# Reordering the normalisation of q and k in an attention and soft-MoE kernel: q squared one quad earlier, transposes moved forward, norm moved on VectorE

## The chip, the cores and the metric

The kernel runs on one core of a Trainium2 chip. The metric is device time in microseconds (us) of one execution. A profile comes from one execution, and its span is about 1.8 us shorter than that execution's device time (301.9 against 303.69 us before the change). Unless said otherwise, all runs compared are fast.

## The reference, cut to what matters

```python
def rmsnorm(x, g):
    rms = np.sqrt(np.mean(x * x, axis=-1, keepdims=True) + 1e-06)
    return x / rms * g
# attention: batch 8, 12 heads, 448 tokens, head size 64
q_n, k_n = rmsnorm(q, g_q), rmsnorm(k, g_k)
attn = softmax(q_n @ k_n.T / sqrt(64));  x = attn @ v        # x: 3584 x 768
# soft MoE: 8 experts of 4 slots, 768 -> 1024 -> 768
logits = x @ phi
slot_input = softmax(logits over tokens).T @ x
slot_out = per expert: relu(slot_input @ w1) @ w2
out = softmax(logits over slots) @ slot_out
```

Only the factors 1/rms and the order in which they are made concern us.

## The kernel before

The attention works on quads (four heads), 24 of them, three to a batch. Quad Q is scored while k and q of quad Q+1 are transposed and those of quad Q+2 are normalised. In the trace of this kernel each engine's instructions stand in the order of the program text (seen from 118 to 127 us): in the turn that begins at 120.59 us TensorE runs score 0 (120.59), 12 ov matmuls (120.97), score 1 (121.44), 8 of ov (121.82), score 2 (122.13), 8 of ov (122.51), 7 transposes of q (122.76) and score 3 (123.78). One turn of the loop, with cuts:

```python
if on: score(Q, 0)               # PE: two matmuls; ACT: exp
if ahead:
    square(Q + 2, 0)             # ACT: q*q
    if Q: square(Q + 2, 1, True) # POOL: k*k
ov(Q - 1, 1, 7, 10)              # PE: attn @ v, half 1 of the quad before
moe_evac(moe)                    # DVE: copy of x transposed (xT)
score(Q, 1); ov(Q - 1, 1, 10, 12)
rowsum(Q + 2, 0)                 # DVE: sum of q*q
# if mb (last quad of a batch): logits on PE, exp on ACT
score(Q, 2); ov(Q - 1, 1, 12, 14)
trans(Q + 1, 0); evac(Q + 1, 0)  # PE: 7 transposes of q; DVE: evacuation
rowsum(Q + 2, 1)                 # DVE: sum of k*k
score(Q, 3)
norm(Q - 1, 1)                   # DVE: divides half 1 of ov, frees the accumulator
trans(Q + 1, 1); vcopy(Q + 1)    # PE: 8 transposes of k; POOL: casts of v
rsqrt(Q + 2)                     # ACT: Ln, Exp = "factor pass", 28 columns
scaleqk(Q + 2, 0); scaleqk(Q + 2, 1)   # POOL
score(Q, 4); ov(Q, 0, 0, 4)      # waits for norm(Q - 1, 1): one ov accumulator
evac(Q + 1, 1)                   # DVE: two copies, partitions 0-63 and 64-127
score(Q, 5); ov(Q, 0, 4, 7)
# if mb: moe_sin: expert sums and transposes of e on PE, sacc and eT on DVE
score(Q, 6); norm(Q, 0); moe_x(Q - 1)
```

PSUM holds two score tiles, one ov accumulator and two slots ("misc") for transposes and small tiles. A score must wait until the exp two scores back has emptied its slot: score 3 waited 0.47 us for exp 1 in the turn above, and started at 123.78 us, 0.96 us after that exp did.

The softmax here doesn't subtract the row's maximum and nothing guards it: scores larger than these inputs give would overflow.

## Time and profile before

| | before |
|---|---|
| device time, median of 3 (range) | 303.25 us (302.88 to 305.39) |
| span of the profiled run | 301.9 us |
| attention part / expert and output tail | 229 / 73 us |
| plain quad, norm to norm of half 1 | 8.12 us |
| third quad (with expert sums) | 10.2 to 10.5 us |

A fourth run of this kernel (303.02 us) came with the runs of the changed kernel; the medians below include it. Times of quads are read as the distance between two starts of the norm of half 1 on VectorE (DVE) in the timeline. "Third quad" here is the stretch that follows the norm in a quad that ends a batch, because the expert sums lie in it. The first norm of half 1 is that of quad 0; it runs in turn 1 of the loop, so some texts call it the norm of quad 1, and a stretch between two norms is called by the turn in which it ends. Two lines from the table of waits of the kernel before; the columns are who waited, for whom, us in total, times, longest:

```profile
DVE ss L186 <- ACT arena L180: 27.6, 19, 2.3
...
ACT ss L190 <- DVE ss L186: 12.6, 24, 3.8
```

VectorE's sum waits for Square on ScalarE (ACT), and ScalarE's factor pass waits for the sum. The change aims at the first.

### The profile page before, as it was taken

To read this page: it belongs to the slowest core of one execution; us is meant where nothing else is said; L and a number is where in the kernel's file an instruction comes from. 1 tells how busy PE (TensorE), PEld (TensorE's weight loads), DVE (VectorE), ACT (ScalarE), POOL (GpSimd) and SP (SyncE) were. 2 spreads that over 40 slices of the span, in tenths; PEclk is the share of its full clock that TensorE was granted. 3 is DMA by queue.
4 is the path that set the end of the run, shared out by engine and by line. 5 is a ranking of instruction groups with operands and counts; after the bars stand their busy time and mean duration, and the time that the engine had idled before them with its cause. 6 is when DMAs were issued, how large, how long until landed. Compare 5 with 4: busy or idle time off the path is not lost.

```text
span 301.9 us, 8426 instructions
## 1 busy us (share of the span) xinstructions
PE 219.0 (73%) x3564; PEld 157.8 (52%) x3564; DVE 189.8 (63%) x315; ACT 193.3 (64%) x270; POOL 167.4 (55%) x187
## 2 busy tenths in 40 slices
PE   7568878687877867787788589686976756689900
PEld 2244556455655645565556456554745746654300
DVE  5765777887777788777767877877555300038800
ACT  4388988778878877887867889687771000026700
POOL 0389999767968885978776689779502100000000
PEclk9969999999999999999979999999998555555555
DMA  6996999999999899999994998939999999209996
GB/s 194 280 285 175 243 265 251 272 241 252 244 243 267 236 212 270 220 258 280 232 236 129 227 263 205 226 104 154 212 211 214 209 212 211 55 2 396 405 414 247
DMA packets 44918, 69.81 MB, mean 231 GB/s; under 512 B 3920, under 2 KB 36688, under 8 KB 44880
## 3 DMA queue, kind: packets, MB, share of 16 engines
q1 hardware_dynamic: 29184, 44.05, 48.9%
q0 software_dynamic: 15376, 25.22, 46.1%
q8 instruction: 28, 0.46, 0.6%
q14 instruction: 10, 0.08, 0.1%
q10 hardware_dynamic: 320, 0.00, 0.1%
HBM read 83.46 MB, written 11.01 MB: 313 GB/s over the span
## 4 chain that ended last, share of the span: by engine, by line
PE 36%; DVE 33%; ACT 17%; issue 5%; DMA 3%; POOL 1%; SPq 0%; POOLq 0%; DVEq 0%
DVE ss L186 13%; ACT arena L243 11%; PE ov L256 11%; PE sc L242 8%; DVE arena L267 7%; DVE eT L310 5%; ACT arena L180 4%; PE hTp L444 4%; PE soTp L453 4%; PE op L483 3%; DVE arena L223 3%; PE sinp L298 2%; DMA arena<-in_v_dram 2%; PE op L484 2%; DVE rd L266 2%
## 5 line engine op out<-in xcount | busy, mean ns | idle before, releaser
L243 ACT ACTIVATE arena<-sc 128x896 bf16<-128x896 f32 x168 | 146.2, 916 | 28.0 <-PE sc L242 27.7
L242 PE MATMUL sc<-arena 128*128 128x448 bf16 x336 | 93.2, 360 | 10.2 <-ACT arena L243 9.1
L198 POOL TENSOR_TENSOR arena<-arena,rs 128x896 bf16<-128x896 f32 x47 | 79.6, 1714 | 35.0 <-issue 19.3
L256 PE MATMUL ov<-arena 128*128 128x65 bf16 (+1 forms) x1344 | 67.2, 199 | 40.7 <-DVE arena L267 40.6
L256 PEld LDWEIGHTS <-arena 128*128 128x128 bf16 x1344 | 59.1, 99 | 71.3 <-DVE arena L267 43.5
L186 DVE TENSOR_REDUCE ss<-arena 128x14 f32<-128x896 f32 x48 | 51.8, 1080 | 28.1 <-ACT arena L180 27.6
L487 ACT ACTIVATE wown<-op,arena 128x768 f32<-128x768 f32 x14 | 12.4, 899 | 42.3 <-PE op L484 42.3
L178 POOL TENSOR_TENSOR arena<-arena 128x896 f32<-128x896 f32 x21 | 35.4, 1687 | 0.2
L267 DVE TENSOR_TENSOR arena<-ov,rd 128x512 bf16<-128x512 f32 x48 | 33.2, 691 | 1.7
L242 PEld LDWEIGHTS <-arena 128*128 128x128 bf16 x336 | 25.7, 98 | 14.5 <-issue 11.5
L227 DVE COPY arena<-qkTp 64x896 bf16<-64x896 bf16 x48 | 29.6, 616 | 0.6
L216 PE MATMUL qkTp<-ident,arena 128*128 128x128 bf16 x360 | 28.7, 223 | 0.4 <-DVE arena L198 0.4
L180 ACT ACTIVATE arena<-arena 128x896 f32<-128x896 f32 x27 | 25.4, 942 | 3.4 <-DMA arena<-in_q_dram 2.2
L216 PEld LDWEIGHTS <-arena 128*128 128x128 bf16 x360 | 23.2, 100 | 5.8 <-issue 0.7
L223 DVE TENSOR_SCALAR arena<-qkTp,gg 128x896 bf16<-128x896 bf16 x24 | 16.2, 675 | 5.4 <-PE qkTp L216 5.3
L266 DVE RECIPROCAL rd<-ov 128x8 f32<-128x8 f32 x48 | 10.0, 207 | 13.3 <-PE ov L256 13.2
L489 DVE TENSOR_SCALAR wown<-op,arena 128x768 f32<-128x768 f32 x14 | 14.1, 1016 | 4.6 <-PE op L484 4.4
L281 DVE COPY arena<-xTp 128x1024 bf16<-128x1024 bf16 x24 | 16.3, 680 | 1.1 <-PE xTp L278 1.1
L483 PE MATMUL op<-arena,eT 32*128 32x512 bf16 x28 | 16.0, 616 | 1.4 <-ACT wown L487 0.7
L205 POOL CAST arena<-arena 128x384 bf16<-128x384 f32 x24 | 12.1, 505 | 8.4 <-PE ov L256 8.3
L190 ACT ACTIVATE ss<-ss,eps 128x28 f32<-128x28 f32 (+1 forms) x26 | 8.2, 316 | 12.6 <-DVE ss L186 12.6
L278 PEld LDWEIGHTS <-arena 128*128 128x128 bf16 x192 | 12.9, 99 | 5.6 <-DVE arena L267 1.1
(62 smaller groups left out, 207.8 us busy)
## 6 DMA issues: line engine op xcount, KB each, us to landing
wown<-in_moe_w_dram POOLq DMA_DIRECT2D x11, 1536.0 KB, 14.2
arena<-in_q_dram SPq DMA_DIRECT2D x24, 448.0 KB, 6.5
arena<-in_k_dram SPq DMA_DIRECT2D x24, 448.0 KB, 8.1
out_dram<-wown SPq DMA_DIRECT2D x12, 768.0 KB, 9.0
arena<-in_moe_w_dram POOLq DMA_DIRECT2D x5, 1536.0 KB, 17.8
arena<-in_v_dram SPq DMA_DIRECT2D x48, 128.0 KB, 6.5
arena<-in_v_dram SPq DMA_DIRECT2D x48, 96.0 KB, 7.5
out_dram<-wown SPq DMA_DIRECT2D x4, 384.0 KB, 8.9
```

The lines of the kernel that those rows point to most:

```text
L178: nc.gpsimd.tensor_tensor(sq(t), r, r, op=MUL)
L180: nc.scalar.activation(out=sq(t), in_=r, func=ACTF.Square)
L186: nc.vector.reduce_sum(sss[Q][:, t], sq(t).rearrange("p (r d) -> p r d", d=D), axis=AX)
L198: (eng or nc.gpsimd).tensor_tensor(qkn(Q, t).rearrange("p s (r d) -> p s r d", r=2), raw(Q)[:, t].rearrange("p r (s d) -> p s r d", d=D), ...
L216: nc.tensor.transpose(pts[t][:, i], qkn(Q, t)[:, s], ident)
L223: nc.vector.tensor_scalar(qT(Q).rearrange("p w (s c) -> p w s c", s=NT), pt[:, :, :NT], gg, None, op0=MUL)
L227: nc.vector.tensor_copy(kT(Q)[r, :, hh].rearrange("p w (s c) -> p w s c", s=NT), pt[r, :, 1 - hh:8 - hh])
L242: nc.tensor.matmul(sc[:, j, :S], kT(Q)[:, w].rearrange("p h c -> p (h c)")[:, kc:kc + 128], qT(Q)[:, w], start=True, stop=True)
L243: nc.scalar.activation(out=at("attn", i).rearrange("p (h c) -> p h c", h=2), in_=sc[:, :, :S], func=ACTF.Exp, scale=0.125)
L256: nc.tensor.matmul(ovs[w][:, c, o0:o0 + n], attn(i)[:, C0[c]:C0[c] + 128], mov, start=(first and i == lo and c % 2 == 0), stop=(i in (6, 13)),
L267: nc.vector.tensor_tensor(xq(Q).rearrange("p c (h w d) -> p c h w d", h=2, w=2)[:, :, :, w], o[:, :, :, :D], rd.to_broadcast([128, 4, 2, D ...
L483: nc.tensor.matmul(op[:, 0], eTtok(j, s), so4[r, :512], start=True, stop=True, tile_position=tp)
```

## The change

Its intent: the sum of q no longer waits for a Square of the same quad, the transposes come early enough for their evacuations to be out of the way, and the norm, which frees the ov accumulator, no longer stands behind the sum of k. The diff, cut to its core (the split of the raw buffer into four q slots and three k slots, the index change of the factor tiles to Q+t, and one weight load moved from quad 20 to 21 are left out):

```diff
-    for t in range(2):              # prologue
-        square(0, t)
-        rowsum(0, t)
-    for t in range(2):
-        rsqrt(0, t, t + 1)
+    square(0, 0)
+    rowsum(0, 0)
+    square(0, 1)
+    rsqrt(0, 0, 1)
+    square(1, 0)
+    rowsum(1, 0)
+    rowsum(0, 1)
+    rsqrt(1)                        # k of quad 0 and q of quad 1
 ...
-    for t in range(2):
-        square(1, t)
-        rowsum(1, t)
-        rsqrt(1, t, t + 1)
-        scaleqk(1, t)
+    scaleqk(1, 0)
+    square(1, 1)
+    square(2, 0)
+    rowsum(1, 1)
+    rowsum(2, 0)
+    rsqrt(2)
+    scaleqk(1, 1)
 ...
         score(Q, 0)
+        square(Q + 3, 0)
-        square(Q + 2, 0)
         square(Q + 2, 1, ...)
+        trans(Q + 1, 0); evac(Q + 1, 0)
         ov(Q - 1, 1, 7, 10); moe_evac(moe)
+        scaleqk(Q + 2, 0)
         score(Q, 1); ov(Q - 1, 1, 10, 12)
+        trans(Q + 1, 1); evac(Q + 1, 1)
+        rowsum(Q + 3, 0)
-        rowsum(Q + 2, 0)
         score(Q, 2); ov(Q - 1, 1, 12, 14)
-        trans(Q + 1, 0); evac(Q + 1, 0)
-        rowsum(Q + 2, 1)
         score(Q, 3); norm(Q - 1, 1)
-        trans(Q + 1, 1)
         vcopy(Q + 1)
-        rsqrt(Q + 2); scaleqk(Q + 2, 0); scaleqk(Q + 2, 1)
+        rowsum(Q + 2, 1)
         score(Q, 4); ov(Q, 0, 0, 4)
-        evac(Q + 1, 1)
+        rsqrt(Q + 3, ...); scaleqk(Q + 2, 1)
```

More of the change, by code (lines that the diff above doesn't have):

```diff
@@ L68, in place @@
         places[name] = (off, elems, n)
-    place("raw", 2 * 2 * 2 * NT * D, 3)
+    place("rawq", 2 * 2 * NT * D, 4)
+    place("rawk", 2 * 2 * NT * D, 3)
     place("sq", 2 * 2 * 2 * NT * D, 1)
@@ L102, in loadw, with raw @@
         nc.gpsimd.dma_start(out=wt[i], in_=wsrc(i))
-    def raw(Q):
-        return at("raw", Q).bitcast(F32).rearrange("p (t r x) -> p t r x", t=2, r=2)
+    def raw(Q, t):
+        return at(("rawq", "rawk")[t], Q).bitcast(F32).rearrange("p (r x) -> p r x", r=2)
     def load(Q, t):
         src = (q, k)[t][Q // QB, Q % QB * 4:Q % QB * 4 + 4].rearrange("h t d -> (h t) d")
-        nc.sync.dma_start(out=raw(Q)[:, t], in_=src.rearrange("(r p s) d -> p r (s d)", r=2, s=NT))
+        nc.sync.dma_start(out=raw(Q, t), in_=src.rearrange("(r p s) d -> p r (s d)", r=2, s=NT))
     def vraw(Q):
@@ L174, in square @@
     def square(Q, t, pool=False):
-        r = raw(Q)[:, t].rearrange("p r x -> p (r x)")
+        r = raw(Q, t).rearrange("p r x -> p (r x)")
         if pool:
@@ L182, in rowsum, with rsqrt @@
     def rowsum(Q, t):
-        if t == 0:
-            sss[Q] = small.tile([128, 2, 2 * NT], F32, tag="ss", name="ss")
-            rss[Q] = small.tile([128, 2, 2 * NT], F32, tag="rs", name="rs")
-        nc.vector.reduce_sum(sss[Q][:, t], sq(t).rearrange("p (r d) -> p r d", d=D), axis=AX)
-    def rsqrt(Q, t0=0, t1=2):
-        ss, rs = sss[Q][:, t0:t1], rss[Q][:, t0:t1]
+        n = Q + t
+        if n not in sss:
+            sss[n] = small.tile([128, 2, 2 * NT], F32, tag="ss", name="ss")
+            rss[n] = small.tile([128, 2, 2 * NT], F32, tag="rs", name="rs")
+        nc.vector.reduce_sum(sss[n][:, t], sq(t).rearrange("p (r d) -> p r d", d=D), axis=AX)
+    def rsqrt(n, t0=0, t1=2):
+        ss, rs = sss[n][:, t0:t1], rss[n][:, t0:t1]
         nc.scalar.activation(out=ss, in_=ss, func=ACTF.Ln, scale=1.0 / D, bias=eps)
@@ L196, in scaleqk @@
     def scaleqk(Q, t, eng=None):
-        rs = rss[Q][:, t].rearrange("p (r s) -> p s r", r=2)
+        rs = rss[Q + t][:, t].rearrange("p (r s) -> p s r", r=2)
         (eng or nc.gpsimd).tensor_tensor(qkn(Q, t).rearrange("p s (r d) -> p s r d", r=2),
-                                         raw(Q)[:, t].rearrange("p r (s d) -> p s r d", d=D),
+                                         raw(Q, t).rearrange("p r (s d) -> p s r d", d=D),
                                          rs.to_broadcast([128, NT, 2, D]), op=MUL)
@@ L325 @@
     evac(0, 1)
-    for t in range(2):
-        square(1, t)
-        rowsum(1, t)
-        rsqrt(1, t, t + 1)
-        scaleqk(1, t)
+    scaleqk(1, 0)
[5 more added lines that the diff above has]
+    scaleqk(1, 1)
     vcopy(0)
-    WQ = [0, 2, 4, 6, 9, 11, 13, 16, 18, 20, 20, 21, 22, NQ, NQ]
+    WQ = [0, 2, 4, 6, 9, 11, 13, 16, 18, 20, 21, 21, 22, NQ, NQ]
     for Q in range(NQ + 2):
@@ L345 @@
             score(Q, 0)
+        if Q + 3 < NQ:
+            square(Q + 3, 0)
         if ahead:
-            square(Q + 2, 0)
-            if Q:
-                square(Q + 2, 1, True)
+            square(Q + 2, 1, Q > 0)
+        if Q + 1 < NQ:
+            trans(Q + 1, 0)
+            evac(Q + 1, 0)
         if 0 <= Q - 1 < NQ:
@@ L353 @@
             moe_evac(moe)
+        if ahead:
+            scaleqk(Q + 2, 0)
         if on:
@@ L358 @@
             ov(Q - 1, 1, 10, 12)
-        if ahead:
-            rowsum(Q + 2, 0)
-            if Q == 0:
-                square(2, 1)
+        if Q + 1 < NQ:
+            trans(Q + 1, 1)
+            evac(Q + 1, 1)
+        if Q + 3 < NQ:
+            rowsum(Q + 3, 0)
         if mb is not None:
@@ L369 @@
             ov(Q - 1, 1, 12, 14)
-        if Q + 1 < NQ:
-            trans(Q + 1, 0)
-            evac(Q + 1, 0)
-        if ahead:
-            rowsum(Q + 2, 1)
         if on:
@@ L380 @@
         if Q + 1 < NQ:
-            trans(Q + 1, 1)
             vcopy(Q + 1)
         if ahead:
-            rsqrt(Q + 2)
-            scaleqk(Q + 2, 0)
-            scaleqk(Q + 2, 1)
+            rowsum(Q + 2, 1)
         for q3 in (2, 3) if Q == 0 else (Q + 3,):
@@ L393 @@
             ov(Q, 0, 0, 4)
-        if Q + 1 < NQ:
-            evac(Q + 1, 1)
+        if ahead:
+            rsqrt(Q + 3, 0 if Q + 3 < NQ else 1)
+            scaleqk(Q + 2, 1)
         if on:
```

## The prediction

> **What bounds the kernel now.** I read the page's first two parts, then the table of stretches, the chain of waits, and last the timeline of one quad (a quad is four heads; 24 of them pass through the loop). No engine is full:
>
> ```profile
> PE 219.0 (73%) x3564; PEld 157.8 (52%) x3564; DVE 189.8 (63%) x315; ACT 193.3 (64%) x270; POOL 167.4 (55%) x187
> ...
> PEclk9969999999999999999979999999998555555555
> ```
>
> The shares mix an attention part (to about 229 us) with a tail of expert layers and output that the change leaves alone, 73 us long. In the table of stretches the attention part alone, 60 to 203 us, shows ScalarE busy 116.45 of 143 us, TensorE 110.69, VectorE 110.03, GpSimd 109.66: four engines near 80%, none at its limit, so the order in which they wait decides. The chain of waits between 118 and 128 us shows that order for one plain quad:
>
> ```profile
> 117.66 0.70 DVE arena L267
> 118.36 0.05 issue
> 118.41 0.66 PE ov L256 x16
> 119.07 0.39 PE sc L242 x2
> 119.46 0.02 issue
> 119.48 2.60 ACT arena L243 x3
> 122.08 0.85 ACT arena L180
> 122.93 0.02 issue
> 122.95 1.09 DVE ss L186
> 124.04 0.59 DVE arena L223
> 124.63 0.99 DVE ss L186
> 125.62 0.13 DVE rd L266
> 125.75 0.02 issue
> 125.77 0.70 DVE arena L267
> 126.47 0.05 issue
> 126.52 0.67 PE ov L256 x16
> 127.19 0.39 PE sc L242 x2
> ```
>
> It is a ring: norm (L267) to norm takes 125.77 - 117.66 = 8.11 us. The norm frees the one ov accumulator, 16 ov matmuls run, score 5 follows, then exp 5, exp 6, exp 0 of the next quad and Square of q on ScalarE, then on VectorE sum of q, evacuation of q (L223), sum of k, norm. In that ring ScalarE waits twice:
>
> ```profile
> 125.66 0.32 ACT L190 ACTIVATE ss<-ss,eps 128x28 f32<-128x28 f32 x1 [0.32 <-DVE ss L186]
> 126.07 0.23 ACT L191 ACTIVATE rs<-ss 128x28 f32<-128x28 f32 x1
> 126.20 0.90 ACT L243 ACTIVATE arena<-sc 128x896 bf16<-128x896 f32 x1
> 127.60 2.60 ACT L243 ACTIVATE arena<-sc 128x896 bf16<-128x896 f32 x3 [0.51 <-PE sc L242]
> ```
>
> 0.32 us before the factor pass (Ln and Exp) and 0.51 us after exp 5: 0.83 us of 8.12. So ScalarE needs 7.29 us a quad and the most that any reordering can win in a plain quad is 0.83 us. Every third quad (the last of a batch) also holds the expert sums and the 1.90 us copy to eT (L310). In the chain three quads take 26.7 us (norm at 90.96 to norm at 117.66), so such a quad takes 26.7 - 2 x 8.12 = 10.4 us.
>
> [...] each engine's timeline has the kernel's order, and the norm at 125.77 stands behind a sum that it does not need. So I may follow queues by hand. [...] Here the gaps repeat, and there is one ov accumulator and two slots each for score tiles and small PSUM tiles. [...] the 48 sums last 1073 to 1087 ns whatever GpSimd does.
>
> **The change part by part.** (a) No work is added or removed in a steady quad: still two squares, two sums, one Ln/Exp pair of 28 columns, the same transposes. (b) Square of q is done for quad Q+3, of k for Q+2, and the pass takes both together; it moves from behind exp 3 to behind exp 4. (c) On TensorE the transposes of q follow score 0 and those of k follow score 1 (both followed score 2 and 3). (d) On VectorE the built order becomes: evacuation of q, copy of xT (L281), evacuation of k (two copies), sum of q, norm of half 1, sum of k, norm of half 0. Before: xT, sum q, evacuation q, sum k, norm, evacuation k, norm. So the norm passes only the sum of k; the sum of q still precedes it, and the evacuation of k (1.26 us), which used to follow, now precedes it too.
>
> What (b) wins: the old ring is cut, as the sum of q no longer waits for this quad's Square in time to matter. What (c) and (d) build is a new ring. The factor pass stands on ScalarE before exp 5 and needs the sum of k. In VectorE's order that sum comes after everything from the evacuation of q on. The evacuation needs the q transposes, which stand behind score 0, and score 0 needs the score slot that exp 5 of the previous quad frees. Each hop with a duration from this trace, start to start:
> 1. score 0 (two matmuls) until the transposes start: 0.38 (119.76 to 120.14, sc to the next transposes).
> 2. seven transposes until the evacuation of q starts: 0.59 (141.94 to 142.53, VectorE waiting).
> 3. evacuation of q: 0.59 (123.96 to 124.55).
> 4. xT copy 0.68 plus 0.06 to wake TensorE (norm end 126.46 to ov 126.52): 0.74. The k transposes need this: the small PSUM tiles have two slots, and theirs is the slot that the xT tile holds until it is copied. The built program has such a wait of TensorE on VectorE there.
> 5. eight transposes until the evacuation of k starts: 0.61 + 0.04 = 0.65.
> 6. two copies: 1.29 (11.31 to the next sum at 12.60).
> 7. sum of q: 0.99 (124.55 to 125.54).
> 8. norm: 0.23 + 0.61 = 0.84 (125.54, 125.77, 126.38).
> 9. sum of k 1.09 plus 0.03 to wake ScalarE: 1.12.
> 10. Ln and Exp until exp 5 starts: 0.54 (125.66 to 126.20).
> 11. exp 5 until score 0 may start: 0.96 (122.82 to 123.78).
> Sum 8.69 us, against 8.12 now: +0.57 per plain quad. The same way of adding gives the old ring exactly: 2.50 (exp 5, 6, 0) + 0.97 + 1.01 + 0.59 + 0.99 + 0.23 + 0.75 + 0.50 + 0.58 = 8.12, which is why I trust it. Other paths fit inside: score 5 is ready 1.14 us after the norm's end while exp 5 is released only at 1.59; ScalarE then idles about 1.4 us ahead of each factor pass.
>
> Third quads: sacc, eT and the norm of half 0 come after the sum of k. Counted from the end of the norm of half 1, the evacuation of the next q starts 3.52 us later in a plain quad, but 5.50 in a third one (16 ov 0.06, sacc 2.31, eT 2.73, norm 4.65 to 5.50, taken from the third quad at 134.6 to 140.1). That is +1.98, and about 0.1 for the memset of e: 8.69 + 2.08 = 10.77, against 10.4.
>
> Sum over the 20 quads from exp 5 of quad 0 (23.53) to exp 5 of quad 20 (201.20), 177.7 us now, of which I take 1.6 as a dip of the granted clock near 153 us that may come again: 14 x 8.69 + 6 x 10.77 + 1.6 = 187.9, so +10.2. Quad 21 has no sum of q any more (8.69 - 0.99 = 7.70; it now takes 8.7, held by GpSimd with two weight loads): -1.0. The prologue: k's first factors now wait also for q of quad 1, and the first exps for q of quad 2; following the queues I get about +1.0. The tail is unchanged: the weight loads that follow quad 21 still have some microseconds to spare. Total +10.2: 303.25 becomes about 313; I round down to 312.5, since each hop may overlap a little more than I allow.
>
> **The rivals.** First, the intent works: the Square-to-sum wait (27.6 us in 19 waits in the table of waits) goes and ScalarE runs through at 7.29 us; 0.83 x 14 plus about 1.5 x 6 saves some 20 us, giving 283. For it: that wait is the largest of VectorE, and the norm comes one sum earlier relative to k. Against it: the ring above, which is made of queue order and not of speed. Second, a draw: if the k transposes do not wait for the xT copy (hop 4 shrinks by about 0.35), or the two copies overlap, the ring is 8.2 to 8.3 and the time 304 to 307. Third, GpSimd becomes the bound: per quad 3 x 1.69 + 1.8 of casts, plus 0.94 for a weight load, 6.9 to 7.8 us; below 8.69, so it would only cap the first rival. Fourth, transfers: q must now be there a quad earlier, by my count 11.7 us after its issue; the landings of q and k have a median of 7.3 and a maximum of 13.3, so a rare wait is possible, and adds perhaps 1 to 3 us.
>
> **Range and chances.** An error of 0.25 us in the ring is 20 x 0.25 = 5 us, a different prologue or clock dip 2 us; so 306 to 318. The 2% lines lie at 297.2 and 309.3. Below 309.3 needs a ring under about 8.5; below 297.2 needs the ring not to exist. Slower 0.73, same 0.21, faster 0.06.
>
> **What would show it.** Right: norm to norm of half 1 near 8.7 us in plain quads; the wait of the Ln for the sum of k grows from 0.32 to above 1 us per quad (now 12.6 us in 24 waits, 4.9 of it between 60 and 203 us; then above 25); the wait of the sum of q for Square all but vanishes; in the chain the evacuations of q and k, xT and both sums stand in a row, and exp time shrinks to one exp per quad. Wrong: the norm of half 1 following the k evacuation with no sum before it, k transposes running ahead of the xT copy, or ScalarE with no repeated gap ahead of the factor pass.

## The result, and the profile after

| | before | after |
|---|---|---|
| device time, median of 4 (range) | 303.13 us (302.88 to 305.39) | 313.22 us (311.51 to 315.0) |
| span of the profiled run | 301.9 us | 309.7 us |
| plain quad | 8.12 us | 8.37 to 8.40 us |
| third quad | 10.2 to 10.5 us | 10.5 to 10.7 us |
| first norm of half 1 (turn 1 of the loop) | 29.92 us | 32.55 us |

The ratio is 1.0316 (95% interval 1.0239 to 1.0393). Here and below a ratio is the mean time of one kernel's fast runs over that of the kernel before in the same rounds, so it is not quite the ratio of the medians.

The kernel became 3% slower, though it does the same work. The page of the changed kernel:

```profile
PE 225.3 (73%) x3564; PEld 160.1 (52%) x3564; DVE 196.3 (63%) x315; ACT 191.9 (62%) x268; POOL 165.2 (53%) x187
```

The numbers of instructions are those of the kernel before, but for two fewer on ScalarE, so no work was added, though TensorE and VectorE show 3% more busy time: it is the order. The table of waits:

```profile
ACT ss L193 <- DVE ss L189: 31.2, 23, 4.8
...
DVE ss L189 <- ACT arena L181: 3.0, 2, 2.8
```

The wait that the change aimed at fell from 27.6 to 3.0 us, as intended. In exchange ScalarE's wait for the sums, ahead of the factor pass, grew from 12.6 to 31.2 us. The chain of waits of one plain quad shows why (columns: start, us, engine, tile, line):

```profile
125.60 0.69 DVE arena L270
126.29 1.00 DVE ss L189
...
127.32 0.33 ACT ss L193
...
127.95 0.81 ACT arena L246
...
128.81 0.54 PE sc L245 x2
129.35 0.39 PE qkTp L219 x7
129.74 0.48 PE ov L259 x12
130.22 0.38 PE sc L245 x2
130.60 0.24 PE ov L259 x8
130.84 0.46 PE qkTp L219 x8
...
131.32 0.62 DVE arena L230
...
132.61 1.09 DVE ss L189
...
133.97 0.69 DVE arena L270
```

Read from the top: norm (L270), sum of k (L189), factor pass (L193 and one more), exp 5 (L246), score 0 of the next quad (L245), transposes of q (L219), then on TensorE's own queue 12 ov matmuls, score 1 and 8 ov matmuls, transposes of k, evacuation of k (L230, two halves), sum of q, reciprocal, norm. 133.97 - 125.60 = 8.37 us. Before, this chain had three exps and a Square in a row; now it has one exp. It is a ring that the new order closes: ScalarE's queue has the factor pass ahead of exp 5, VectorE's queue has the sum of k behind the evacuations, and TensorE's queue has the transposes behind score 0.

Where the 7.8 us between the two profiled spans are, by the starts of the norms (differences of the two timelines):

| stretch | before | after | difference |
|---|---|---|---|
| until the first norm of half 1 | 29.92 | 32.55 | +2.6 |
| 13 plain quads, without their excess | 105.6 | 109.0 | +3.4 |
| 6 third quads | 62.3 | 63.9 | +1.6 |
| excess of long quads (see below) | 1.6 | 2.7 | +1.1 |
| turns 21 to 23 | 24.3 | 23.1 | -1.2 |
| last quad and tail | 78.3 | 78.5 | +0.2 |

Long quads are single quads that take 1.3 to 1.6 us more than their kind while the granted clock is low. In the table of stretches of the changed kernel (columns: us, busy time of PE, PEld, DVE, ACT, POOL, granted clock, DMA share, GB/s), this is the stretch of the first of two such quads, which took 9.70 and 9.73 us (32.6 to 52.0 us):

```profile
30.00:40.00 10.00, 8.27 (x103) 5.87 (x101) 6.70 (x11) 7.91 (x11) 8.76 (x10) 0.83 1.08 231
```

The granted clock is 0.83 there, and 1.00 from 50 us on. The profiled run was the fastest of the four (311.51 us), so the median of 10.1 us above before holds some 2 us that this trace does not show.

### The profile page after: what moved, and what is told of

The parts are those of the page before. It is cut to its first block, busy times and chain, and to the rows that moved or that the text cites. A ratio compares the mean times of both kernels' runs of the same rounds, so it can differ in the third digit from the quotient of the medians.

```text
span 309.7 us, 8398 instructions
## 1 busy us (share of the span) xinstructions
PE 225.3 (73%) x3564; PEld 160.1 (52%) x3564; DVE 196.3 (63%) x315; ACT 191.9 (62%) x268; POOL 165.2 (53%) x187
## 4 chain that ended last, share of the span: by engine, by line
PE 42%; DVE 33%; ACT 9%; issue 7%; DMA 3%; POOL 1%; SPq 0%; ACTq 0%; POOLq 0%
DVE ss L189 11%; PE ov L259 11%; PE sc L245 10%; DVE arena L270 7%; ACT arena L246 6%; PE qkTp L219 6%; DVE arena L230 6%; DVE eT L313 5%; PE hTp L451 3%; PE op L490 3%; PE soTp L460 3%; DVE rd L269 2%; PE sinp L301 2%; DMA arena<-in_k_dram 2%; PE op L491 2%
## 5 line engine op out<-in xcount | busy, mean ns | idle before, releaser
L246 ACT ACTIVATE arena<-sc 128x896 bf16<-128x896 f32 x168 | 144.0, 919 | 17.5 <-PE sc L245 15.6
L201 POOL TENSOR_TENSOR arena<-arena,rs 128x896 bf16<-128x896 f32 x47 | 81.4, 1733 | 57.5 <-ACT rs L194 48.1
L245 PE MATMUL sc<-arena 128*128 128x448 bf16 x336 | 94.8, 365 | 13.0 <-ACT arena L246 9.4
L259 PEld LDWEIGHTS <-arena 128*128 128x128 bf16 x1344 | 60.1, 99 | 54.3 <-DVE arena L270 35.4
L189 DVE TENSOR_REDUCE ss<-arena 128x14 f32<-128x896 f32 x48 | 51.6, 1081 | 3.7 <-ACT arena L181 3.0
L245 PEld LDWEIGHTS <-arena 128*128 128x128 bf16 x336 | 26.5, 100 | 25.4 <-issue 20.7
L230 DVE COPY arena<-qkTp 64x896 bf16<-64x896 bf16 x48 | 29.8, 622 | 11.6 <-PE qkTp L219 11.3
L219 PE MATMUL qkTp<-ident,arena 128*128 128x128 bf16 x360 | 29.2, 225 | 9.8 <-POOL arena L201 3.1
L270 DVE TENSOR_TENSOR arena<-ov,rd 128x512 bf16<-128x512 f32 x48 | 33.2, 692 | 1.7
L219 PEld LDWEIGHTS <-arena 128*128 128x128 bf16 x360 | 23.4, 101 | 16.9 <-issue 6.4
L193 ACT ACTIVATE ss<-ss,eps 128x28 f32<-128x28 f32 (+1 forms) x25 | 7.9, 316 | 31.2 <-DVE ss L189 31.2
L269 DVE RECIPROCAL rd<-ov 128x8 f32<-128x8 f32 x48 | 10.2, 213 | 17.5 <-PE ov L259 16.6
L281 PEld LDWEIGHTS <-arena 128*128 128x128 bf16 x192 | 13.3, 101 | 5.9 <-DVE arena L270 1.2
L281 PE MATMUL xTp<-ident,arena 128*128 128x128 bf16 x192 | 15.2, 224 | 1.0 <-DVE arena L270 1.0
```

Of the source, the lines that this page charges most:

```text
L189: nc.vector.reduce_sum(sss[n][:, t], sq(t).rearrange("p (r d) -> p r d", d=D), axis=AX)
L201: (eng or nc.gpsimd).tensor_tensor(qkn(Q, t).rearrange("p s (r d) -> p s r d", r=2), raw(Q, t).rearrange("p r (s d) -> p s r d", d=D), rs. ...
L219: nc.tensor.transpose(pts[t][:, i], qkn(Q, t)[:, s], ident)
L230: nc.vector.tensor_copy(kT(Q)[r, :, hh].rearrange("p w (s c) -> p w s c", s=NT), pt[r, :, 1 - hh:8 - hh])
L245: nc.tensor.matmul(sc[:, j, :S], kT(Q)[:, w].rearrange("p h c -> p (h c)")[:, kc:kc + 128], qT(Q)[:, w], start=True, stop=True)
L246: nc.scalar.activation(out=at("attn", i).rearrange("p (h c) -> p h c", h=2), in_=sc[:, :, :S], func=ACTF.Exp, scale=0.125)
```

## The experiments

All twelve kernels gave correct results.

**Norm ahead of both sums.** The change was meant to put the norm ahead of the sums; in the built order it precedes only the sum of k.

```diff
         evac(Q + 1, 1)
-        rowsum(Q + 3, 0)
 ...
         score(Q, 3); norm(Q - 1, 1); vcopy(Q + 1)
+        rowsum(Q + 3, 0)
         rowsum(Q + 2, 1)
```

> The changed kernel with the sum of q moved behind the norm of half 1, so that the norm really precedes both sums. Theory (the ring runs through both sums, the factor pass and exp 5, whatever the order of sums and norm on VectorE): the plain quad goes from 8.37 us to about 8.24 [...], time 309 to 313. Rival (the wait of the 16 ov matmuls for the norm sets the pace, as it did before the change): the norm comes a sum (about 1.1 us) earlier, the plain quad falls to about 7.3 and the time below 298.

(The 0.13 us from 8.37 to 8.24 is the difference between 1.12 us from sum to reciprocal in the changed kernel and 0.99 in the kernel before; the experiment with the two halves, below, looks at it.) Measured: plain quads 8.24 us, as the theory said (8.37 in turns ahead of a third quad, once 8.76); but the time was 304.03 us (ratio 1.0046, 0.9995 to 1.0096), lower than the theory and above the rival. The rival's ring is not there. What I had left out were the third quads, which fell from 10.48 to 9.38 us and later from 10.73 to 9.6. VectorE's timeline in a third quad holds sacc, the addition of the expert sums; the bracket at the end of the line gives VectorE's idle time before it and what ended it. First the changed kernel, then this one:

```profile
145.36 0.39 DVE L306 TENSOR_TENSOR sacc<-sinp,sacc 128x224 f32<-128x224 f32 x1 [1.31 <-PE sinp L301]
```

```profile
137.96 0.39 DVE L306 TENSOR_TENSOR sacc<-sinp,sacc 128x224 f32<-128x224 f32 x1 [0.32 <-PE sinp L301]
```

Between the norm and sacc VectorE must wait for the expert sums of TensorE, which start from the norm. In the changed kernel 1.31 us of that hole were idle; here the sum of q fills it (0.32 left), and is gone from the stretch that counts. So in a plain quad the place of a sum relative to the norm does not matter, since both lie in the ring, and in a third quad it is worth a whole sum. The rest of the gain in this trace, 2.7 us, is that it has no long quad. Its first norm comes 1.1 us earlier (31.43 us), but only because a sum no longer stands ahead of it, and turn 21 gives this back (8.25 us against 7.25).

**Transposes of k directly behind those of q.** The copy of xT goes ahead of both evacuations, so this moves two things, and both shorten the same hop.

```diff
         square(Q + 2, 1, Q > 0)
+        moe_evac(moe)
         trans(Q + 1, 0); evac(Q + 1, 0)
+        trans(Q + 1, 1); evac(Q + 1, 1)
         ov(Q - 1, 1, 7, 10)
-        moe_evac(moe)
 ...
         score(Q, 1); ov(Q - 1, 1, 10, 12)
-        trans(Q + 1, 1); evac(Q + 1, 1)
```

> The changed kernel with the k transposes directly behind the q transposes (both behind score 0) and the xT copy ahead of the q evacuation on VectorE. Theory of the ring: the stretch from q evacuation to k evacuation falls from 1.54 us to about 0.74 (then held by the scaled k that GpSimd delivers 1.0 us after score 0 starts), so the plain quad goes from 8.37 to about 7.6 and the third quad from 10.6 to about 9.9; time near 298 (294 to 302). Rival (GpSimd, the transfers or ScalarE's own work set the pace of the changed kernel): no gain over 1 per cent, 310 or more.

Measured: plain quads mostly 7.57 to 7.61 us, third quads 10.02 to 10.23, time 299.81 us (ratio 0.9893, 0.9834 to 0.9952). From evacuation of q to evacuation of k it is now 0.75 us:

```profile
122.35 0.68 DVE L226 TENSOR_SCALAR arena<-qkTp,gg 128x896 bf16<-128x896 bf16 x1 [0.34 <-PE qkTp L219]
123.10 1.26 DVE L230 COPY arena<-qkTp 64x896 bf16<-64x896 bf16 x2
```

Shortening this one hop by 0.79 us shortened the plain quad by as much, with the work of every engine unchanged, so the rival falls for the changed kernel. In this version the chain of waits does run through GpSimd's scaling of k (1.72 us), as the theory said it would. Three plain quads were longer (8.66, 7.81 and 8.58 us in turns 3, 4 and 7); ScalarE's Squares waited here for transfers of q for 9.0 us in 10 waits, against 2.4 us in 2 in the changed kernel. Which of the longer quads that explains was not tested.

**The old order in the loop, with the new squares and prologue.** The loop of the kernel before, except that q is squared and summed for quad Q+3 and the pass takes q of Q+3 with k of Q+2. The edit, against the changed kernel:

```diff
         score(Q, 0); square(Q + 3, 0); square(Q + 2, 1, Q > 0)
-        trans(Q + 1, 0); evac(Q + 1, 0)
         ov(Q - 1, 1, 7, 10); moe_evac(moe)
-        scaleqk(Q + 2, 0)
         score(Q, 1); ov(Q - 1, 1, 10, 12)
-        trans(Q + 1, 1); evac(Q + 1, 1)
         rowsum(Q + 3, 0)
         score(Q, 2); ov(Q - 1, 1, 12, 14)
+        trans(Q + 1, 0); evac(Q + 1, 0); rowsum(Q + 2, 1)
         score(Q, 3); norm(Q - 1, 1)
+        trans(Q + 1, 1)
         vcopy(Q + 1)
-        rowsum(Q + 2, 1)
+        rsqrt(Q + 3, ...); scaleqk(Q + 2, 0); scaleqk(Q + 2, 1)
         score(Q, 4); ov(Q, 0, 0, 4)
-        rsqrt(Q + 3, ...); scaleqk(Q + 2, 1)
+        evac(Q + 1, 1)
```

> The changed kernel's squares a quad ahead, joint factor pass and prologue, but in the loop the old places of transposes, evacuations, sums, norm and factor pass. Theory: squaring q ahead changes nothing by itself, plain quads return to 8.1 us; what is left over the kernel before is the prologue (norm of quad 1 about 2.6 us later) and whatever the clock does at the start (0 to 3 us): 305 to 309. Rival (squaring ahead itself costs, by later loads of q or by the joint pass): plain quads stay near 8.4 and the time above 311.

Measured: plain quads 8.11 to 8.13 us but for one long one, third quads 10.2 to 10.5, as before the change; first norm at 33.70 us; time 306.84 us (ratio 1.0131, 1.0094 to 1.0169). Squaring ahead by itself neither wins nor costs in the loop. What remains of the loss is the prologue (3.8 us later here).

**The norm alone, in the kernel before.**

```diff
         trans(Q + 1, 0); evac(Q + 1, 0)
-        rowsum(Q + 2, 1)
         score(Q, 3); norm(Q - 1, 1)
+        rowsum(Q + 2, 1)
```

> The kernel before with one part of the change alone: the norm of half 1 ahead of the sum of k. Theory: the old ring loses the sum (0.99 us), but the factor pass ahead of exp 4 then comes 0.85 us later and makes a ring of its own of about 8.4 us: plain quads 8.4, time 306 to 310, a little slower than before. Rival (the intent: the norm freed of the sum starts ov earlier and that is what counts): plain quads near 7.3, time below 292.

Both theories missed. Plain quads took 8.27 to 8.29 us, longer than before, as the ring of the factor pass said, though by less (it had 8.4), but the time was 297.93 us (ratio 0.9827, 0.9798 to 0.9856). The third quads fell from 10.22 to 9.24 us and later from 10.46 to 9.47. Before, and with this edit:

```profile
136.90 0.39 DVE L303 TENSOR_TENSOR sacc<-sinp,sacc 128x224 f32<-128x224 f32 x1 [1.14 <-PE sinp L298]
```

```profile
133.80 0.39 DVE L303 TENSOR_TENSOR sacc<-sinp,sacc 128x224 f32<-128x224 f32 x1 [0.15 <-PE sinp L298]
```

It is the same hole (1.14 us), filled by the sum of k. Of the 5.8 us between the two profiled spans (301.9 and 296.1), the third quads won 5.9 and the plain ones lost 2.1; another 1.6 is that this trace has no long quad, and an earlier first norm (-1.6) and longer turns 21 to 23 (+1.1) partly cancel. One line of the change, taken alone, is thus a gain over the kernel before; it is the other parts that lose.

**The two halves of the evacuation of k swapped.** In the changed kernel a sum is followed by the reciprocal after 1.12 us; in the kernel before it was 0.99. After the change the last instruction ahead of the sum is the copy that starts at partition 64; in the kernel before it was the evacuation of q, which starts at partition 0. My guess was that this lengthens the hops that follow, and the edit tests it.

```diff
-            for hh in range(2):
+            for hh in (1, 0):
                 r = slice(64 * hh, 64 * hh + 64)
```

> The changed kernel with the two halves of the k evacuation in the other order (partitions 64 to 127 first), so that VectorE's last read of PSUM and last write of SBUF before the sum and the norm start at partition 0. Theory [...]: sum of q to reciprocal goes from 1.12 to 0.99 us and second copy to sum from 0.66 to about 0.61; plain quad 8.37 to about 8.2, 3 to 4 us in all. Rival (the 0.13 us is the reciprocal's wait for TensorE): nothing changes.

Measured: 305.82 us (ratio 1.0082, 1.0048 to 1.0117), plain quads 8.12 us. VectorE's timeline of the changed kernel and of this one:

```profile
131.32 1.26 DVE L230 COPY arena<-qkTp 64x896 bf16<-64x896 bf16 x2 [0.26 <-PE qkTp L219]
132.61 1.09 DVE L189 TENSOR_REDUCE ss<-arena 128x14 f32<-128x896 f32 x1
133.73 0.21 DVE L269 RECIPROCAL rd<-ov 128x8 f32<-128x8 f32 x1
```

```profile
128.82 1.26 DVE L230 COPY arena<-qkTp 64x896 bf16<-64x896 bf16 x2 [0.26 <-PE qkTp L219]
130.00 1.07 DVE L189 TENSOR_REDUCE ss<-arena 128x14 f32<-128x896 f32 x1
131.00 0.19 DVE L269 RECIPROCAL rd<-ov 128x8 f32<-128x8 f32 x1
```

First copy to sum fell from 1.29 to 1.18 us, sum to reciprocal from 1.12 to 1.00. Only the order of the two copies differs, so the two hops are longer, by 0.11 and 0.12 us, when the copy that starts at partition 64 comes last. Why, the traces don't show. The loop gains 0.25 us in every quad, plain or third (0.11 at the first hop, where I had expected 0.05): some 5 us in 19 stretches. The other 2.5 us of the 7.5 between this median and that of the unchanged kernel in the same call (313.31) I cannot assign for all runs; in the two profiled runs, one long quad fewer accounts for 1.3 us, and a shorter last quad and tail (78.3 us against 79.1) for 0.8; the first norm (33.24 us) did not gain. Such a small edit undoes nearly the whole loss of the ring (8.37 back to 8.12).

**Filling TensorE's gaps at the start.** Quads 2 and 3 were long in the first trace, with the clock at 0.83; from 15 to 25 us it was 0.50, with TensorE busy for 6.09 of the 10 us.

```diff
+    fill(8)                  # idle matmuls on a constant tile
     scaleqk(1, 0)
 ...
+    if Q == 0: fill(16)
     trans(Q + 1, 1)
```

> The changed kernel with 24 idle matmuls on a constant tile put into TensorE's gaps of the prologue (8 before score 0 of quad 0, 16 before its k transposes); they feed nothing. Theory (TensorE's idle time in the prologue lowers the granted clock for the first quads): clock near 1.0 from about 25 us on, norms of quads 1 to 4 about 25.5 us apart, time 2 to 4 us below the unchanged kernel of the same call. Rival (the clock at the start has another cause, or chance): no difference beyond 1 us, or a loss by the added matmuls.

Measured: 311.64 us (ratio 1.0256, 1.0161 to 1.0351), against 313.31 us of the unchanged kernel in the same call (1.0364, 1.0284 to 1.0444): the intervals overlap. One of its four runs, the profiled one, is slow, so only counts are taken from it: the clock was 1.0 from 20 to 40 us, but the quad from 42.0 to 51.7 us took 9.71 us all the same, and two more long quads came at 161 and 182 us; the first norm stood at 33.66 us, no earlier. The theory that the idle prologue makes the first quads long is not borne out, nor is it settled: of the three fast runs two, with a mean granted clock of 0.873 and 0.874, took 309.9 and 309.0 us, and the third, with 0.859, took 313.4.

**The changed kernel again, twice, and the kernel before again.**

> The changed kernel once more, unchanged, for its start: in its first trace the granted clock stayed near 0.5 from 15 to 25 us and near 0.84 until 50 us, and quads 2 and 3 took 9.7 us instead of 8.4. If that belongs to the kernel (idle TensorE in the longer prologue), it comes again: norms of quads 1 to 4 about 27.8 us apart in all, time 311 to 315. If it was chance, about 25.5 us and a time near 310.

> The changed kernel a third time, for the same count: 2 or more long quads if the dips belong to it, 0 or 1 if they are chance. Plain quads without a dip 8.37 us, third quads 10.5 to 10.7 us, in any case.

> The kernel before once more, for its clock: how many quads are longer than their kind by about 1.35 us while the granted clock dips. Its first trace had one such dip (near 155 us) after the start. If the changed kernel draws more dips than this one (it showed two in each of two traces), this trace has 0 or 1; if dips are chance, 2 or more here are as likely.

The first repeat took 313.31 us (median of 4). The other two were single looks, of unknown state: 315.26 us, and 302.75 us for the kernel before. In the first repeat the norms of turns 1 to 4 were 26.5 us apart, between the two figures expected. Long quads: the changed kernel had 2, 2 and 4 in its three traces, at different places (turns 2, 3; 2, 15; 4, 6, 16, 18), the kernel before 1 and 1 (its first norms stood at 29.92 and 30.69). Plain quads of the changed kernel were 8.36 to 8.40 us and third quads 10.47 to 10.74 in all three, first norms at 32.55, 33.43 and 33.10. So a long quad is not bound to a place. All traces with plain quads of 8.36 to 8.40 us, those of this kernel and of the fill and prologue experiments, have 2 to 4 of these dips; the old order and the swapped halves have 1 each, and the others (norm ahead, k with q, norm alone, both combined versions) none after their first turns. So the changed order seems to draw more of them; most kernels have one trace only, so this is not shown. By its busy time and its longest wait TensorE was no idler in the dips than elsewhere: in the two long quads of the first trace (32.6 to 52.0 us, clock 0.82) it was busy for 15.96 of 19.4 us (82%) and waited at most 1.8 us at a time, and from 60 to 200 us of that trace (clock 1.00) for 108.03 of 140 us (77%), with waits of at most 2.0 us. The cause of the dips stays open.

**The prologue eased.** k of quad 0 takes its factors alone, and so do k of quad 1 and q of quad 2.

```diff
-    square(1, 0)
-    rowsum(1, 0)
     rowsum(0, 1)
-    rsqrt(1)
+    rsqrt(1, 1, 2)
+    square(1, 0)
     scaleqk(0, 0); trans(0, 0); scaleqk(0, 1, nc.vector); trans(0, 1)
+    rowsum(1, 0)
+    rsqrt(1, 0, 1)
 ...
-    rsqrt(2)
+    rsqrt(2, 1, 2)           # k of quad 1 alone
 ...
         square(Q + 3, 0)
+        if Q == 0: rsqrt(2, 0, 1)    # q of quad 2: behind the first exp
```

> The changed kernel with only its prologue eased: k of quad 0 takes its factors by itself, without q of quad 1, and the first exp does not wait for the sum of q of quad 2. Theory (the prologue of the change costs 2.4 to 2.6 us, besides and apart from the ring): first exp about 16.5 instead of 19.1 us, norm of quad 1 near 30.1 instead of 32.5 to 33.4 us, plain quads unchanged at 8.37, time 2 to 3 us below the changed kernel, 309 to 312. Rival (the time lost at the start is made up later, in transfers or the tail): same time, 313.

Measured: first exp at 15.68 us, first norm at 30.33 us (32.5 to 33.4 in the changed kernel's traces), plain quads 8.37: the 2.2 to 3.1 us of the prologue are found where they were expected. The time, 311.88 us (ratio 1.0297, 1.0206 to 1.0387), is below the changed kernel's, but the intervals overlap. The trace had four long quads (9.71, 9.72, 9.75 us, and 8.61 where 7.25 is usual), so that trace had lost again what it had won; that the easing lowers the time is not shown.

**Two versions that put the findings together.** The first takes k transposes with q, norm ahead of both sums, swapped halves and the eased prologue.

> All that the theory of the ring offers at once: both transposes behind score 0 with the xT copy first, norm of half 1 ahead of both sums, halves of the k evacuation swapped, and a prologue in which k of quad 0 gets its factors without waiting for q of quad 1, and the first exp without waiting for q of quad 2. Theory: plain quads 7.4 to 7.6 us (ScalarE's own work is 7.29), third quads 8.4 to 8.9, norm of quad 1 near 29.5 us; time 281 to 287, better than both kernels. Rival (GpSimd with up to 7.9 us in a quad with a weight load becomes the bound): plain quads 7.8 to 8.0, time 289 to 294.

Measured: 299.91 us over 20 runs, one of them slow (ratio 0.9901, 0.9875 to 0.9927), above what both theory and rival said. Plain quads took 7.88 us (8.5 in most turns ahead of a third quad): the rival's figure, and the chain names the engine; third quads took 9.4 to 9.7, not 8.4 to 8.9.

```profile
119.75 0.24 ACT rs L194
...
120.12 1.72 POOL arena L201
...
121.89 0.62 PE qkTp L219 x8
```

The ring now leads from the factor pass over GpSimd's scaling of k (1.72 us) to the transposes of k and on through TensorE's queue to the norm, which waits for the last ov matmuls (0.46 us in the timeline). It is not GpSimd's total work but its place in a ring: GpSimd itself waits for the factors, 42.5 us in 22 waits. With norm first, VectorE has nothing to do in that wait; in the second experiment the sum of q filled it, and plain quads were 7.58. So the second version lets the sum of q lead in plain quads and follow in third quads (the diff is against the changed kernel; the parts of the first version stay):

```diff
-        if Q + 3 < NQ:
+        if Q + 3 < NQ and mb is None:
             rowsum(Q + 3, 0)
-        if mb is not None: moe_logits(mb)
 ...
         ov(Q - 1, 1, 12, 14)
+        if mb is not None: moe_logits(mb)
 ...
         norm(Q - 1, 1); vcopy(Q + 1)
+        if Q + 3 < NQ and mb is not None: rowsum(Q + 3, 0)
         rowsum(Q + 2, 1)
```

> Both transposes behind score 0, xT copy first, halves swapped, eased prologue; the sum of q stays ahead of the norm in plain quads (where VectorE would otherwise wait for ov) and goes behind it in third quads (where it fills the wait for the expert sums); the logits move behind the last ov matmuls of a half. Theory: plain quads 7.4 to 7.5 us, third quads 9.0 to 9.4, time 284 to 291, the fastest of all. Rival (TensorE's queue or GpSimd takes over as in the version before, where plain quads stayed at 7.88): 295 to 300.

Measured: plain quads 7.33 us, which is close to ScalarE's own 7.29; third quads 9.74 to 10.0, more than expected; time 297.58 us (ratio 0.9795, 0.9743 to 0.9847), well above the 284 to 291 of the theory and within the rival's range. The turns ahead of a third quad also took mostly 7.95 to 8.5 us instead of 7.33, and the norm there waited for TensorE (1.55 us in the quad at 130 us). In turn 7, 9.04 us long, the chain runs through a transfer of q that took 9.45 us. It beats both kernels, by 2% of the kernel before, but no more than the one-line edit above does (0.9827; the intervals overlap).

## Why the prediction was right or wrong

Right was that a new ring through the three in-order queues would cost more than the removed wait, and three of the signs named for it came: ScalarE's wait ahead of the factor pass rose from 12.6 to 31.2 us ("above 25"; 1.25 and 1.45 us in single quads), the Square wait all but vanished, exp time in the chain shrank to one exp. Two did not: the plain quad is not near 8.7 us, and the evacuation of q and the copy of xT don't stand in the chain, which takes TensorE's queue instead. The total, 312.5 us against 313.22, is nearer than the steps deserve:

- Ring, +0.57 us predicted, +0.25 to 0.28 measured. Step 4 of the sum, that the k transposes wait for "the slot that the xT tile holds until it is copied", failed. In the changed kernel:

```profile
129.78 0.68 DVE L226 TENSOR_SCALAR arena<-qkTp,gg 128x896 bf16<-128x896 bf16 x1 [0.94 <-PE qkTp L219]
...
130.38 0.68 DVE L284 COPY arena<-xTp 128x1024 bf16<-128x1024 bf16 x1
...
130.67 0.61 PE L219 MATMUL qkTp<-ident,arena 128*128 128x128 bf16 x8
```

  The k transposes start 0.29 us after the xT copy began and long before it ended at 131.06, so they do not wait for it. They come when TensorE's own queue reaches them, behind ov, score 1 and ov, and after the evacuation of q (ended 130.46); of the two slots it must thus be that of q which they take. Evacuation of q to evacuation of k took 131.32 - 129.78 = 1.54 us, where steps 3 to 5 gave 0.59 + 0.74 + 0.65 = 1.98. I had named "k transposes running ahead of the xT copy" as a sign that I was wrong, and it came. Step 7 erred the other way: 1.12 us instead of 0.99; with the two halves swapped it was 1.00. The two together (-0.44 + 0.13) are the difference between 8.69 and 8.37, but for 0.01.
- Third quads: 10.77 predicted, 10.5 to 10.7 measured. The mechanism, everything from sacc to the next evacuation behind the norm, was right; that VectorE idles 1.3 us there I had not used, and it made me miss the two experiments in which a sum fills that hole.
- Prologue: +1.0 predicted, +1.9 to +3.5 measured at the first norm (32.55 to 33.43 us in three traces, against 29.92 and 30.69 in two). The term was mis-sized: in the first traces the first exp started at 19.13 us instead of 16.73, behind a factor pass that waited for both sums of its pair.
- Quad 21: -1.0 predicted. Turn 21 took 7.25 us instead of 8.72; turns 21 to 23 together brought -1.2.
- Dips of the granted clock: one expected in both kernels; the changed kernel had 2 to 4 of about 1.35 us. This and the prologue make up for the ring that was reckoned 0.3 us too long over 20 quads.

Of the rivals, the draw had the nearer ring and the right reason (k transposes not waiting for xT; 8.2 to 8.3 against 8.37), and lost by the prologue and the dips. GpSimd did not bound this kernel, but did enter the ring once that ring was shortened. The transfers did not bound it either: ScalarE's Squares waited 2.4 us in all for q, against 2.2 before; in four of the faster versions (norm ahead, k with q, swapped halves, second combined one) this wait is 8.1 to 9.0 us, so it is the next thing to look at.

## What to carry to other kernels

When no engine is full, write down each engine's queue and look for the ring: follow one instruction through the queues until you come back to it a turn later, and add the start-to-start times. Moving work earlier on one engine helps only if it leaves the ring; a reorder that removes the largest wait can close a longer ring elsewhere (here a wait of 27.6 us in all fell to 3.0, and the plain quad grew from 8.12 to 8.37 us). Do this for each kind of turn, the rare ones too, and fill with movable work the holes in which an engine must wait anyway: one line that filled a hole of 1.1 us in every third quad was worth more than the whole rearrangement.
